# A mixer kernel on one core: the first product of the MLP, for three pairs of token chunks, by seven block products in place of eight

## Chip, cores, metric

The kernel runs on 1 core of one Trainium2 chip. The metric is device time in microseconds (us) of one execution. Before the change the median of 3 runs is 878.2 us (876.82 to 881.63).

## What is computed

Eight sequences of 576 tokens go through windowed attention (8 heads of 64), and the result, 512 wide, through a mixer: a product over the tokens with a ReLU, then an MLP over the channels with a residual. The change is in the MLP, the last three lines.

```python
x = attn_out.transpose(0, 2, 1, 3).reshape(B, S, H * D)   # 8 x 576 x 512
xt = x.transpose(0, 2, 1)
h = np.maximum(xt @ w_tok1, 0.0) @ w_tok2                  # 576 -> 256 -> 576, over tokens
u = x + h.transpose(0, 2, 1)
h2 = np.maximum(u @ w_ch1, 0.0) @ w_ch2                    # 512 -> 1536 -> 512, over channels
return u + h2
```

## The kernel before

**Two stages.** The first stage (to about 283 us) does attention and the token product, writes u to DRAM in 9 chunks of 512 tokens (`u_dram[j]`, 128 partitions x 4 channel tiles x 512 tokens), and converts the weights from float64, in DVE, ACT and POOL work spread over its steps as "jobs". The second stage, from line 539, is the MLP, chunk by chunk (`for j in range(NCHUNK)`, line 585).

**Split numbers.** Every operand of the MLP is held as two float32r tiles, a rounded part `hi` (made by an ACT copy) and the rest `lo` (made by a DVE subtraction, line 94). A product of two such operands is three matmuls: hi by hi, hi by lo, lo by hi.

**A chunk.** The first product, which makes `gp`, goes over 12 tiles `ft` of the 1536 hidden channels. Each is 4 channel tiles x 3 = 12 matmuls of 128x512 into one PSUM bank (line 593). ACT's ReLU takes it out as `ghi` (line 597) and DVE makes `glo` (line 598). The banks come in turn from the tags "s" and "pt", two each, so PE can be four tiles ahead. The second product, `op`, goes over 4 output tiles `ct`, each 12 x 3 = 36 matmuls (line 629), in banks of other tags. DVE adds the residual (line 631) and SP stores the tile (line 632). So a chunk is 144 + 144 matmuls. The last output tile of the last chunk is done in two halves of 256 columns, in two banks (`LAST_PARTS`). The next chunk's u is loaded after tile 3 and split after tile 8 (lines 608 to 611).

**Chunk 0** also holds the rest of the conversion of the second weight matrix: twelve pieces (`late_steps`, line 568, two steps after each tile and seven ahead of each output tile) and three that were kept in DRAM (`load_w2`, `split_w2`). Their DVE work stands in DVE's queue between the `glo` of this chunk.

**Order.** Each engine works its queue in the order in which the program issues it; the schedule is written out by hand. SP issues all DMAs here, in order, and one that waits holds up those behind it.

**Memory.** Pools lie one behind the other, and a pool's tiles follow the order of their first use. A tile that lies where an older tile lay waits for that tile's readers alone (`reuse_waits="tile"`). Pool `pa` (first stage) is followed at the same place by `pb` (MLP).

Of the kernel before, what the change touches and what calls it, by code (L numbers as in the profile page):

```python
# [20 lines left out]
B, H, S, D = 8, 8, 576, 64  # L21
C = H * D
P = 128
# [6 lines left out]
F = 1536  # L30
NCT = C // P
NFT = F // P
NTT = DT // P
TOK = B * S
CHUNK = 512
CW = 384

LAST_PARTS = 2
# [10 lines left out]

NX = 4  # L50
NCHUNK = TOK // CHUNK
NEG = -1.0e9

NEG_PE = -2.0 ** 33
# [20 lines left out]
def mixer_kernel(ctx: ExitStack, tc: tile.TileContext, qh, kh, vh, wt1, wt2, wc1, wc2, out):  # L75
    nc = tc.nc
# [3 lines left out]
    dram = ctx.enter_context(tc.tile_pool(name="dram", bufs=1, space=bass.MemoryType.DRAM))  # L80
    ps = ctx.enter_context(tc.tile_pool(name="ps", bufs=2, space=PSUM))

    ident = const.tile([P, P], F32, name="ident")
    w1hi = const.tile([P, NCT * F], F32R, name="w1hi")
    w1lo = const.tile([P, NCT * F], F32R, name="w1lo")
    w2_dram = dram.tile([P, NFT * C], F32, name="w2_dram")
    u_dram = [dram.tile([P, NCT, CHUNK], F32, name=f"u_dram{j}") for j in range(NCHUNK)]

    def split(eng_hi, eng_lo, hi, lo, src):
        if eng_hi is nc.scalar:  # L90
            nc.scalar.copy(hi, src)  # L91
        else:
            eng_hi.tensor_copy(hi, src)
        eng_lo.tensor_sub(lo, src, hi.bitcast(F32))  # L94

    def load_u(j, pu):
        uf = pu.tile([P, NCT, CHUNK], F32, name=f"uf{j}", tag="uf", bufs=3)
        uhi = pu.tile([P, NCT, CHUNK], F32R, name=f"uhi{j}", tag="uhi", bufs=2)
        ulo = pu.tile([P, NCT, CHUNK], F32R, name=f"ulo{j}", tag="ulo", bufs=2)
# [13 lines left out]
    with ExitStack() as actx:  # L113
# [6 lines left out]
        kbs, loaded, cpool = {}, {}, [pq]  # L120
# [46 lines left out]
        abs_of = {}  # L167

        def job_abs():
            if to_convert:  # L170
                n, raw = to_convert[0]
                m = jobs[n][4]
                abs_of[n] = pb.tile([P, CW], I32, name=f"c{n}", tag="cvc", bufs=2)[:, :m]
                high = raw[:, :m].bitcast(F32).rearrange("p (n t) -> p n t", t=2)[:, :, 1]
                nc.scalar.activation(abs_of[n].bitcast(F32), high, AF.Abs)

# [55 lines left out]
        finished = set()  # L232
# [223 lines left out]
        tok1_plan, n = {}, 0  # L456
        for i in range(TOK1_FROM, NT + 1):
            m = min(n + (1 if i < TOK1_SLOW else 2), i)
            tok1_plan[i] = range(n, m)
            n = m  # L460
        qk(0)
        for i in range(-1, NT + 1):
# [64 lines left out]
            if i == NT - 1:  # L527
# [5 lines left out]
                pu = uctx.enter_context(tc.tile_pool(name="pu", bufs=1, side="right", reuse_waits="tile"))  # L533
                ul = {0: load_u(0, pu)}
# [4 lines left out]
    with ExitStack() as bctx:  # L539
        pb = bctx.enter_context(tc.tile_pool(name="pb", bufs=1, reuse_waits="tile"))  # L540

        w2hi = pb.tile([P, NCT, NFT, P], F32R, name="w2hi")
        w2lo = pb.tile([P, NCT, NFT, P], F32R, name="w2lo")

        w2hf, w2lf = (t.rearrange("p t f c -> p (t f c)") for t in (w2hi, w2lo))
        cpool[0] = pb
        first = [(o, C) for o in range(0, jobs[N_FIRST][3], C)]
        w2_raw = []

        def load_w2():  # L550
            if first:
                o, m = first.pop(0)
                raw = pb.tile([P, C], F32, name=f"raww2_{o}", tag="raww2", bufs=2)
# [31 lines left out]
        for j in range(NCHUNK):  # L585
            uf, uhi, ulo = ul.pop(j)
            g = []
            for ft in range(NFT):
                gp = ps.tile([P, CHUNK], F32, name=f"gp{j}_{ft}", tag=("s", "pt")[ft % 2])
                k = 0  # L590
                for ct in range(NCT):
                    for w, x in ((w1hi, uhi), (w1hi, ulo), (w1lo, uhi)):
                        nc.tensor.matmul(gp, w[:, ct * F + ft * P:ct * F + (ft + 1) * P], x[:, ct], start=(k == 0), stop=(k == 3 * NCT - 1))  # L593
                        k += 1
                ghi = pb.tile([P, CHUNK], F32R, name=f"ghi{j}_{ft}", tag="ghi", bufs=NFT)
                glo = pb.tile([P, CHUNK], F32R, name=f"glo{j}_{ft}", tag="glo", bufs=NFT)
                nc.scalar.activation(ghi, gp, AF.Relu)  # L597
                nc.vector.scalar_tensor_tensor(out=glo, in0=gp, scalar=0.0, in1=ghi.bitcast(F32),  # L598
                                               op0=ALU.max, op1=ALU.subtract)
                g.append((ghi, glo))  # L600
                if j == 0:
                    for _ in range(2):
                        next(late, None)
                    if ft in (1, 2, 7):
                        load_w2()
                    if ft in (6, 8, 10):
                        split_w2()
                if ft == 3 and j + 1 < NCHUNK:
                    ul[j + 1] = load_u(j + 1, pu)
                if ft == 8 and j + 1 < NCHUNK:  # L610
                    split_u(ul[j + 1])
            for ct in range(NCT):
                if j == 0:
                    for _ in range(7):
                        next(late, None)
                    assert all(n in finished for n in range(23 + 4 * ct, 27 + 4 * ct))
                tag, bufs = (("h", 2), ("av", 1), ("h", 2), ("up", 1))[ct]

                n_part = LAST_PARTS if j == NCHUNK - 1 and ct == NCT - 1 else 1
                for part in range(n_part):  # L620
                    cols = slice(part * CHUNK // n_part, (part + 1) * CHUNK // n_part)
                    if part:
                        tag, bufs = ("s", "pt")[part % 2], 2
                    op = ps.tile([P, CHUNK], F32, name=f"op{j}_{ct}_{part}", tag=tag, bufs=bufs)[:, cols]
                    k = 0
                    for ft in range(NFT):
                        ghi, glo = g[ft]
                        for w, x in ((w2hi, ghi), (w2hi, glo), (w2lo, ghi)):
                            nc.tensor.matmul(op, w[:, ct, ft], x[:, cols], start=(k == 0), stop=(k == 3 * NFT - 1))  # L629
                            k += 1  # L630
                    nc.vector.tensor_add(uf[:, ct, cols], op, uf[:, ct, cols])  # L631
                    nc.sync.dma_start(out[j, :, ct, cols], uf[:, ct, cols])


# [36 lines left out]
```

## Time and profile before

| | |
|---|---|
| median of 3 runs | 878.2 us |
| the profiled execution, its own time | 880.53 us |
| its span, first to last instruction | 878.7 us |
| granted TensorE clock, mean | 0.993 |
| DVE busy over the span | 378.3 us (43%) |
| ACT busy over the span | 307.5 us (35%) |
| DMA, mean over the span | 96 GB/s |
| MLP: chunk 0 | 283.4 to 352.6 us |
| MLP: chunks 1 to 8 | 352.6 to 875.3 us |

How to read the rows: a timeline row gives the start, the duration, the engine, the line, the operation and its tiles. A row of groups gives the count, then the busy time and the mean of one in ns. A row of the chain of waits gives the start, the length and the work that the end of the program hung on there. A row of waits gives who waited for whom: total us, times, longest. A row of windows gives the busy time of each engine, then the clock that was granted to PE (PEclk), the DMA engines' busy share and GB/s. Matmuls overlap: PE starts the next one before the last has ended, so their step and not their duration is the price of one.

### The profile page before, as it was taken

The numbers are of one execution on the slowest core, as the hardware profiler recorded it, in microseconds if no ns is written. First come the engines' busy times: TensorE is split into PE (matmuls) and PEld (weight loads), VectorE is DVE, ScalarE is ACT, GpSimd is POOL, SyncE is SP. The second block draws the span as 40 slices with busy tenths as digits, with TensorE's granted clock in tenths as the row PEclk, the third lists the DMA queues.
The fourth block names the chain that finished last, engine by engine and source line by source line (L and its number), as shares of the span: only waits on it lengthen the run. The fifth ranks groups of instructions, "written<-read, shape, count | busy, mean of one in ns | idle before, by whom it ended". The sixth has DMA issues, their size and how long they took to land.

```text
span 878.7 us, 14566 instructions
## 1 busy us (share of the span) xinstructions
PE 850.6 (97%) x6002; PEld 702.6 (80%) x6002; DVE 378.3 (43%) x701; ACT 307.5 (35%) x966; POOL 105.3 (12%) x109
## 2 busy tenths in 40 slices
PE   6889999989989999999999999999999999999998
PEld 4668878868879878888888888888888888888887
DVE  5979878878874795220220220220220220220211
ACT  5778777878875341120120220220220220220200
POOL 3433343433332000000000000000000000000000
PEclk9989999999999999999999999999999999999999
DMA  9566667567535531100100100100100101100001
GB/s 322 195 203 229 200 235 244 183 235 246 182 127 167 182 106 57 60 7 30 60 13 24 60 13 25 60 13 25 60 12 31 54 13 39 46 13 37 0 13 37
DMA packets 39907, 84.69 MB, mean 96 GB/s; under 512 B 5281, under 2 KB 18337, under 8 KB 37921
## 3 DMA queue, kind: packets, MB, share of 16 engines
q1 hardware_dynamic: 37728, 81.93, 27.9%
q10 hardware_dynamic: 2112, 1.84, 0.6%
q8 instruction: 47, 0.77, 0.4%
q14 instruction: 20, 0.16, 0.1%
HBM read 64.09 MB, written 19.66 MB: 95 GB/s over the span
## 4 chain that ended last, share of the span: by engine, by line
PE 83%; DVE 8%; ACT 4%; POOL 2%; issue 2%; DMA 1%; POOLq 0%; SPq 0%; DVEq 0%; ACTq 0%
PE op L629 33%; PE gp L593 30%; PE h L358 5%; PE up L400 4%; PE s L266 4%; PE xp L313 3%; PE up L393 2%; POOL xlo L94 2%; PE pp L301 1%; ACT u L405 1%; DVE r L200 1%; DMA u_dram<-u 1%; DVE c L197 1%; ACT xhi L91 1%; ACT e L294 1%
## 5 line engine op out<-in xcount | busy, mean ns | idle before, releaser
L597 ACT ACTIVATE ghi<-gp 128x512 fp32r<-128x512 f32 x108 | 64.5, 597 | 432.2 <-PE gp L593 431.9
L629 PE MATMUL op<-ghi,w2lo 128*128 128x512 f32 (+1 forms) x444 | 170.9, 385 | 1.9 <-DVE w2lo L94 1.9
L629 PE MATMUL op<-glo,w2hi 128*128 128x512 f32 (+1 forms) x444 | 170.9, 385 | 0.0
L629 PE MATMUL op<-ghi,w2hi 128*128 128x512 f32 (+1 forms) x444 | 170.8, 385 | 0.0
L593 PE MATMUL gp<-ulo,w1hi 128*128 128x512 f32 x432 | 168.1, 389 | 0.0
L593 PE MATMUL gp<-uhi,w1hi 128*128 128x512 f32 x432 | 168.1, 389 | 0.0
L593 PE MATMUL gp<-uhi,w1lo 128*128 128x512 f32 x432 | 168.0, 389 | 0.0
L598 DVE SCALAR_TENSOR_TENSOR glo<-gp,ghi 128x512 fp32r<-128x512 f32 x108 | 74.5, 690 | 187.7 <-ACT ghi L597 187.7
L631 DVE TENSOR_TENSOR uf<-op,uf 128x512 f32<-128x512 f32 (+1 forms) x37 | 25.0, 677 | 243.7 <-PE op L629 243.7
L629 PEld LDWEIGHTS op<-ghi,w2lo 128*128 128x128 f32 x444 | 83.9, 189 | 18.8 <-DVE w2lo L94 2.3
L629 PEld LDWEIGHTS op<-ghi,w2hi 128*128 128x128 f32 x444 | 83.8, 189 | 16.6
L629 PEld LDWEIGHTS op<-glo,w2hi 128*128 128x128 f32 x444 | 83.8, 189 | 16.5
L593 PEld LDWEIGHTS gp<-uhi,w1hi 128*128 128x128 f32 x432 | 81.1, 188 | 16.9
L593 PEld LDWEIGHTS gp<-uhi,w1lo 128*128 128x128 f32 x432 | 81.1, 188 | 16.8
L593 PEld LDWEIGHTS gp<-ulo,w1hi 128*128 128x128 f32 x432 | 81.1, 188 | 16.8
L294 ACT ACTIVATE e<-e,nm 128x128 f32<-128x128 f32 x232 | 90.5, 396 | 8.0 <-DVE nm L286 8.0
L94 POOL TENSOR_TENSOR xlo<-x,xhi 128x512 fp32r<-128x512 f32 x32 | 42.9, 1340 | 66.3 <-ACT xhi L91 66.0
L313 PEld LDWEIGHTS xp<-v,pt 128*64 128x64 f32 x1152 | 37.4, 137 | 16.4 <-ACT pt L303 6.3
L266 PE MATMUL s<-k,q 64*64 64x128 f32 x1152 | 43.7, 287 | 2.4 <-DVE c L197 1.9
L313 PE MATMUL xp<-v,pt 128*64 128x64 f32 x1152 | 43.1, 226 | 2.7 <-ACT pt L303 2.4
L294 ACT ACTIVATION_READ_ACCUMULATOR e<-e,nm 128x1 f32 x232 | 44.8, 193 | 0.0
L303 ACT COPY pt<-pp 128x512 f32<-128x512 f32 x72 | 41.8, 587 | 6.4 <-PE pp L301 6.3
(79 smaller groups left out, 1002.7 us busy)
## 6 DMA issues: line engine op xcount, KB each, us to landing
v<-vh SPq DMA_DIRECT2D x36, 512.0 KB, 3.8
raw<-wc SPq DMA_DIRECT2D x32, 384.0 KB, 4.4
q<-qh SPq DMA_DIRECT2D x36, 256.0 KB, 4.6
k<-kh SPq DMA_DIRECT2D x7, 1280.0 KB, 8.0
out<-uf SPq DMA_DIRECT2D x35, 256.0 KB, 2.3
uf<-u_dram SPq DMA_DIRECT2D x8, 1024.0 KB, 5.6
u_dram<-u SPq DMA_DIRECT2D x7, 512.0 KB, 3.7
k<-kh SPq DMA_DIRECT2D x5, 256.0 KB, 6.2
```

What stands on the lines that cost most here:

```text
L94: eng_lo.tensor_sub(lo, src, hi.bitcast(F32))
L266: nc.tensor.matmul(s[u][half * BLK:(half + 1) * BLK, j], qt[r, j, half], kbs[b][r, j, n * BLK:n * BLK + P], start=not on_pe, stop=True, sk ...
L294: nc.scalar.activation(e[:, h], src[:, h], AF.Exp, bias=nm[:, g:g + 1], scale=by, accum_out=sm[:, g:g + 1])
L303: nc.scalar.copy(pt, pp)
L313: nc.tensor.matmul(xp[half * BLK:(half + 1) * BLK, h], pts[h % 2][:, h // 2, half * BLK:(half + 1) * BLK], vt[:, half, h], start=True, sto ...
L358: nc.tensor.matmul(h_ps[b][tt], w[:, o + tt * P:o + (tt + 1) * P], x, start=first and n == 0, stop=last and n == len(combos) - 1)
L400: nc.tensor.matmul(up[:, :n], hx[:, cs], w[:, tt * S + s0:tt * S + s0 + n], start=False, stop=(k == 6), skip_group_check=True)
L593: nc.tensor.matmul(gp, w[:, ct * F + ft * P:ct * F + (ft + 1) * P], x[:, ct], start=(k == 0), stop=(k == 3 * NCT - 1))
L597: nc.scalar.activation(ghi, gp, AF.Relu)
L598: nc.vector.scalar_tensor_tensor(out=glo, in0=gp, scalar=0.0, in1=ghi.bitcast(F32), op0=ALU.max, op1=ALU.subtract)
L629: nc.tensor.matmul(op, w[:, ct, ft], x[:, cols], start=(k == 0), stop=(k == 3 * NFT - 1))
L631: nc.vector.tensor_add(uf[:, ct, cols], op, uf[:, ct, cols])
```

## The change

Chunks 0, 1 and 2 stay plain; chunks 3 to 8 become three pairs. For a pair, the first product is seen as 2x2 blocks (two halves of the input channels, two halves of the hidden channels, two chunks), and is made from seven block products of sums (Winograd's form of Strassen's) in place of eight. For each pair and each of 6 tiles `f` (`pair_f`) PE does 7 products of 2 x 3 = 6 matmuls into four banks, P, Q, R and S; three of the products add into a bank that DVE or ACT has read in between. The second product is done for two `f` at a time, in eight open banks: 96 matmuls after each two `pair_f`.

The sums of u (`sums`, `sum4`, `prep`) are made on DVE and ACT from raw u tiles, once for each pair, during chunk 2 for the first pair and around the last `pair_f` of a pair for the next. The weights' sums are made once, during chunk 1 (`weight_steps`, two steps after each tile), stored to DRAM (`w1s`), with the three blocks that need no sum, and streamed into three slots that take the place of the first weight matrix in SBUF (`load_w1`, 1.84 MB for each `f` and pair).

Chunks 1 and 2 do the second product in two halves of the hidden channels, with a residual add for each. In the MLP's pool the tiles of the conversion of the second weight matrix move to a pool of their own (`pl`) behind the others. The last output tile is done in two halves of one bank. The first weight matrix is laid out by halves of the hidden channels.

```diff
+N_PLAIN = 3
+NH = NFT // 2
+PRODUCTS = ("m1", "m6", "m7", "m5", "m2", "m4", "m3")
+SLOT, NSLOT = NPROD * 2 * P, 3
...
+    w1s = [dram.tile([P, NH, NPROD, 2, P], F32, name=f"w1s{k}") for k in range(2)]
...
-        cpool[0] = pb
+        gx = (pu.tile([P, 4, CHUNK], F32R, name="ghix", tag="c4", bufs=1),
+              pb.tile([P, 4, CHUNK], F32R, name="glox", tag="c6", bufs=1))
+        gbuf = [(pb.tile([P, CHUNK], F32R, name=f"ghi0_{n}", tag="ghi", bufs=8),
+                 pb.tile([P, CHUNK], F32R, name=f"glo0_{n}", tag="glo", bufs=8)) for n in range(8)]
...
+        pl = tctx.enter_context(tc.tile_pool(name="pl", bufs=1))
+        cpool[0] = pl
...
+        def store_w1(m, k, f0, ct, src):
+            nf = src.shape[1] // P
+            nc.sync.dma_start(w1s[k][:, f0:f0 + nf, PRODUCTS.index(m), ct],
+                              src.bitcast(F32).rearrange("p (f c) -> p f c", c=P))
+
+        def weight_steps():
+            for m, half, ct0 in (("m1", 0, 0), ("m2", 0, 2), ("m4", 1, 2)):
+                for ct in range(2):
+                    for k, w in enumerate((w1hi, w1lo)):
+                        o = (half * NCT + ct0 + ct) * NH * P
+                        store_w1(m, k, 0, ct, w[:, o:o + NH * P])
+            yield
+            nf = CW // P
+            for n in range(2 * NH // nf):
+                ct, f0 = n % 2, n // 2 * nf
...
+                def keep(m, x):
+                    hi, lo = (pw.tile([P, CW], F32R, name=f"w{k}_{m}_{n}", tag=f"w{k}", bufs=4) for k in ("hi", "lo"))
+                    split(nc.scalar, nc.vector, hi, lo, x)
+                    for k, t in enumerate((hi, lo)):
+                        store_w1(m, k, f0, ct, t)
+
+                a = whole("wa", 1, ct)
+                s1 = whole("ws", 1, 2 + ct)
+                yield
+                nc.vector.tensor_add(s1, s1, a)
+                c = whole("wb", 0, ct)
+                keep("m5", s1)
+                yield
+                nc.vector.tensor_sub(a, c, a)
+                nc.vector.tensor_sub(c, s1, c)
+                keep("m7", a)
+                keep("m6", c)
+                yield
+                d = whole("wd", 0, 2 + ct)
+                nc.vector.tensor_sub(d, d, c)
+                keep("m3", d)
+                yield
...
+        def pair_f(q, f):
...
+            if more:
+                sums()
+            for n, m in enumerate(PRODUCTS):
+                b, c = bank[into[m]], comb[q, m]
...
+                        nc.tensor.matmul(b, w[:, at], c[:, h, t], start=(n < 4 and k == 0), stop=(k == 5),
...
+                if m == "m1":
+                    nc.scalar.copy(x1, b)
+                elif m == "m6":
+                    nc.vector.tensor_add(x1, b, x1)
+                elif m == "m7":
+                    nc.vector.tensor_add(x2, b, x1)
+                elif m == "m5":
+                    nc.vector.tensor_add(x3, b, x2)
+                    done(1, f + NH, x3)
+                elif m == "m2":
+                    done(0, f, b)
+                elif m == "m4":
+                    nc.vector.tensor_add(x2, b, x1)
+                    done(0, f + NH, x2)
+                else:
+                    nc.vector.tensor_add(x1, b, x1)
+                    done(1, f, x1)
+                if more:
+                    if m == "m4":
+                        sum4()
+                    prep(q + 1, m, 0)
```

`whole` is one DVE add of 128x384; `split` is one ACT copy and one DVE subtraction; `done` is ACT's ReLU and DVE's `glo`; `more` is true in the last `pair_f` of a pair that another pair follows. `into` puts m1 and m2 into P, m6 into Q, m7 and m4 into R, m5 and m3 into S.

More of the change, by code (lines that the diff above doesn't have):

```diff
@@ L172, in job_abs @@
                 m = jobs[n][4]
-                abs_of[n] = pb.tile([P, CW], I32, name=f"c{n}", tag="cvc", bufs=2)[:, :m]
+                abs_of[n] = cpool[0].tile([P, CW], I32, name=f"c{n}", tag="cvc", bufs=2)[:, :m]
                 high = raw[:, :m].bitcast(F32).rearrange("p (n t) -> p n t", t=2)[:, :, 1]
@@ L552, in load_w2 @@
                 o, m = first.pop(0)
-                raw = pb.tile([P, C], F32, name=f"raww2_{o}", tag="raww2", bufs=2)
+                raw = pl.tile([P, C], F32, name=f"raww2_{o}", tag="raww2", bufs=2)
                 nc.sync.dma_start(raw[:, :m], w2_dram[:, o:o + m])
@@ L583, in mixer_kernel @@
         late = late_steps()
[L585 to L589, printed above, removed]
-                k = 0
-                for ct in range(NCT):
-                    for w, x in ((w1hi, uhi), (w1hi, ulo), (w1lo, uhi)):
-                        nc.tensor.matmul(gp, w[:, ct * F + ft * P:ct * F + (ft + 1) * P], x[:, ct], start=(k == 0), stop=(k == 3 * NCT - 1))
-                        k += 1
[L595 to L632, printed above, removed]
@@ new lines, in w1_at, with relu_split, new_g @@
+        def w1_at(ft, ct):
+            o = (ft // NH * NCT + ct) * NH * P + ft % NH * P
+            return slice(o, o + P)
+        def relu_split(hi, lo, src):
+            nc.scalar.activation(hi, src, AF.Relu)
+            nc.vector.scalar_tensor_tensor(out=lo, in0=src, scalar=0.0, in1=hi.bitcast(F32),
+                                           op0=ALU.max, op1=ALU.subtract)
+        def new_g(name):
+            return tuple(pb.tile([P, CHUNK], F32R, name=f"g{k}{name}", tag=f"g{k}", bufs=8) for k in ("hi", "lo"))
@@ new lines, in gemm1, with gemm2 @@
+        def gemm1(j, ft, u, g):
+            _, uhi, ulo = u
+            gp = ps.tile([P, CHUNK], F32, name=f"gp{j}_{ft}", tag=("s", "pt")[ft % 2])
+            k = 0
+            for ct in range(NCT):
+                for w, x in ((w1hi, uhi), (w1hi, ulo), (w1lo, uhi)):
+                    nc.tensor.matmul(gp, w[:, w1_at(ft, ct)], x[:, ct], start=(k == 0), stop=(k == 3 * NCT - 1))
+                    k += 1
+            relu_split(*g, gp)
+        def gemm2(op, ct, fts, gs, first, last, cols=slice(0, CHUNK)):
+            k = 0
+            for ft, (ghi, glo) in zip(fts, gs):
+                for w, x in ((w2hi, ghi), (w2hi, glo), (w2lo, ghi)):
+                    nc.tensor.matmul(op, w[:, ct, ft], x[:, cols], start=(first and k == 0),
+                                     stop=(last and k == 3 * len(gs) - 1), skip_group_check=not (first and last))
+                    k += 1
@@ new lines, in add_out, with new_op @@
+        def add_out(j, uf, ct, op, final, cols=slice(0, CHUNK)):
+            nc.vector.tensor_add(uf[:, ct, cols], op, uf[:, ct, cols])
+            if final:
+                nc.sync.dma_start(out[j, :, ct, cols], uf[:, ct, cols])
+        OP_TAGS = (("h", 2), ("av", 1), ("h", 2), ("up", 1))
+        def new_op(name, ct):
+            tag, bufs = OP_TAGS[ct]
+            return ps.tile([P, CHUNK], F32, name=f"op{name}_{ct}", tag=tag, bufs=bufs)
+        u = ul.pop(0)
+        for ft in range(NFT):
+            gemm1(0, ft, u, gbuf[ft])
+            for _ in range(2):
+                next(late, None)
+            if ft in (1, 2, 7):
+                load_w2()
+            if ft in (6, 8, 10):
+                split_w2()
+            if ft == 3:
+                ul[1] = load_u(1, pu)
+            if ft == 8:
+                split_u(ul[1])
@@ new lines, in mixer_kernel @@
+        for ct in range(NCT):
+            for _ in range(7):
+                next(late, None)
+            assert all(n in finished for n in range(23 + 4 * ct, 27 + 4 * ct))
+            op = new_op("0", ct)
+            gemm2(op, ct, range(NFT), gbuf, True, True)
+            add_out(0, u[0], ct, op, True)
+        tctx.close()
+        pw = tctx.enter_context(tc.tile_pool(name="pw", bufs=1, reuse_waits="tile"))
+        def store_w1(m, k, f0, ct, src):
+            nf = src.shape[1] // P
+            nc.sync.dma_start(w1s[k][:, f0:f0 + nf, PRODUCTS.index(m), ct],
+                              src.bitcast(F32).rearrange("p (f c) -> p f c", c=P))
@@ new lines, in load_w1, with load_raw @@
+        def load_w1(n):
+            if n < (NCHUNK - N_PLAIN) // 2 * NH:
+                o = n % NSLOT * SLOT
+                for k, w in enumerate((w1hi, w1lo)):
+                    nc.sync.dma_start(w[:, o:o + SLOT].bitcast(F32),
+                                      w1s[k][:, n % NH].rearrange("p m t c -> p (m t c)"))
+        pairs = [(j, j + 1) for j in range(N_PLAIN, NCHUNK, 2)]
+        px = []
+        comb, raws = {}, {}
+        def load_raw(q, t):
+            raws.clear()
+            for name, j, ct in (("r11", 0, t), ("r12", 1, t), ("r22", 1, 2 + t), ("r21", 0, 2 + t)):
+                raws[name] = px[0].tile([P, CHUNK], F32, name=f"{name}_{q}_{t}", tag=name, bufs=1)
+                nc.sync.dma_start(raws[name], u_dram[pairs[q][j]][:, ct])
+            for name in ("t1", "t2"):
+                raws[name] = px[0].tile([P, CHUNK], F32, name=f"{name}_{q}_{t}", tag=name, bufs=1)
@@ new lines, in sums, with sum4, prep @@
+        def sums(t3=True):
+            r = raws
+            nc.vector.tensor_sub(r["t1"], r["r12"], r["r11"])
+            if t3:
+                nc.vector.tensor_sub(r["r12"], r["r22"], r["r12"])
+            nc.vector.tensor_sub(r["t2"], r["r22"], r["t1"])
+        def sum4():
+            nc.vector.tensor_sub(raws["r11"], raws["r21"], raws["t2"])
+        SOURCE = {"m1": "r11", "m6": "t2", "m7": "r12", "m5": "t1", "m2": "r21", "m4": "r11", "m3": "r22"}
+        def prep(q, m, t):
+            if (q, m) not in comb:
+                pool = pb if HOME[m] == "c6" else pu
+                comb[q, m] = pool.tile([P, 2, 2, CHUNK], F32R, name=f"{m}_{q}", tag=HOME[m], bufs=1)
+            c = comb[q, m]
+            split(nc.scalar, nc.vector, c[:, 0, t], c[:, 1, t], raws[SOURCE[m]])
@@ new lines, in mixer_kernel @@
+        steps = weight_steps()
+        for j in range(1, N_PLAIN):
+            u, last = ul.pop(j), j == N_PLAIN - 1
+            if last:
+                tctx.close()
+                px.append(bctx.enter_context(tc.tile_pool(name="px", bufs=1, reuse_waits="tile")))
+                load_raw(0, 0)
+            for half in range(2):
+                g = []
+                for ft in range(half * NH, (half + 1) * NH):
+                    g.append(new_g(f"{j}_{ft}"))
+                    gemm1(j, ft, u, g[-1])
+                    if j == 1:
+                        for _ in range(2):
+                            next(steps, None)
+                    if not last and ft == 3:
+                        ul[j + 1] = load_u(j + 1, pu)
+                    if not last and ft == 8:
+                        split_u(ul[j + 1])
+                    if last:
+                        if ft == 1:
+                            sums()
+                            prep(0, "m1", 0)
+                            prep(0, "m6", 0)
+                        if ft == 2:
+                            prep(0, "m7", 0)
+                            prep(0, "m5", 0)
+                            prep(0, "m2", 0)
+                            load_raw(0, 1)
+                        if ft == 6:
+                            load_w1(0)
+                            sums()
+                        if ft in (7, 8):
+                            for m in (("m1", "m6"), ("m7", "m5", "m2"))[ft - 7]:
+                                prep(0, m, 1)
+                        if ft == 9:
+                            sum4()
+                if last and half == 1:
+                    for m in ("m4", "m3"):
+                        prep(0, m, 1)
+                    load_raw(0, 0)
+                    load_w1(1)
+                    load_w1(2)
+                for ct in range(NCT):
+                    op = new_op(f"{j}_{half}", ct)
+                    gemm2(op, ct, range(half * NH, (half + 1) * NH), g, True, True)
+                    add_out(j, u[0], ct, op, half == 1)
+                    if last and half == 1 and ct == 1:
+                        sums(False)
+                        sum4()
+                        for m in ("m4", "m3"):
+                            prep(0, m, 0)
@@ new lines, in mixer_kernel, with banks, done @@
+        BANKS = ((("s", 2), ("s", 2), ("pt", 2), ("pt", 2)), (("av", 1), ("up", 1), ("h", 2), ("h", 2)))
+        def banks(name, odd):
+            return [ps.tile([P, CHUNK], F32, name=f"{name}_{n}", tag=tag, bufs=bufs)
+                    for n, (tag, bufs) in enumerate(BANKS[odd])]
+        def pair_f(q, f):
+            bank = dict(zip("PQRS", banks(f"gp{q}_{f}", f % 2)))
+            into = {"m1": "P", "m6": "Q", "m7": "R", "m5": "S", "m2": "P", "m4": "R", "m3": "S"}
+            x1, x2, x3 = (px[0].tile([P, CHUNK], F32, name=f"x{n}_{q}_{f}", tag=f"x{n}", bufs=2 if n == 1 else 1)
+                          for n in (1, 2, 3))
+            o = (q * NH + f) % NSLOT * SLOT
+            g = {}
+            def done(c, ft, src):
+                g[c, ft] = new_g(f"{pairs[q][c]}_{ft}")
+                relu_split(*g[c, ft], src)
+            more = f == NH - 1 and q + 1 < len(pairs)
+            if more:
+                sums()
+            for n, m in enumerate(PRODUCTS):
+                b, c = bank[into[m]], comb[q, m]
+                order = (1, 0) if q == 0 and m in ("m4", "m3") else (0, 1)
+                k = 0
+                for t in order:
+                    at = slice(o + (n * 2 + t) * P, o + (n * 2 + t + 1) * P)
+                    for w, h in ((w1hi, 0), (w1hi, 1), (w1lo, 0)):
+                        nc.tensor.matmul(b, w[:, at], c[:, h, t], start=(n < 4 and k == 0), stop=(k == 5),
+                                         skip_group_check=True)
+                        k += 1
+                if m == "m1":
[17 more added lines that the diff above has]
+                    if m == "m4":
+                        sum4()
+                    prep(q + 1, m, 0)
+            return g
@@ new lines, in mixer_kernel @@
+        for q, (ja, jb) in enumerate(pairs):
+            ufs = []
+            final = q == len(pairs) - 1
+            for f0 in range(0, NH, 2):
+                gs = []
+                for f in (f0, f0 + 1):
+                    if f == NH - 2 and not final:
+                        load_raw(q + 1, 0)
+                    gs.append(pair_f(q, f))
+                    load_w1(q * NH + f + NSLOT)
+                    if f == 1:
+                        for j in (ja, jb):
+                            uf = pu.tile([P, NCT, CHUNK], F32, name=f"uf{j}", tag="uf", bufs=2)
+                            nc.sync.dma_start(uf, u_dram[j])
+                            ufs.append(uf)
+                last = f0 == NH - 2
+                if last and not final:
+                    load_raw(q + 1, 1)
+                outs = [(c, ct) for c in range(2) for ct in range(NCT)]
+                ops = banks(f"op{q}_{f0}a", 0) + banks(f"op{q}_{f0}b", 1)
+                for (c, ct), op in zip(outs, ops):
+                    fts = (f0, f0 + NH)
+                    gemm2(op, ct, fts, [gs[0][c, ft] for ft in fts], True, False)
+                if last and not final:
+                    sums()
+                    for m in PRODUCTS:
+                        if m == "m4":
+                            sum4()
+                        prep(q + 1, m, 1)
+                for (c, ct), op in zip(outs, ops):
+                    fts = (f0 + 1, f0 + 1 + NH)
+                    n_part = LAST_PARTS if final and last and (c, ct) == outs[-1] else 1
+                    for part in range(n_part):
+                        cols = slice(part * CHUNK // n_part, (part + 1) * CHUNK // n_part)
+                        gemm2(op[:, cols], ct, fts, [gs[1][c, ft] for ft in fts], False, True, cols)
+                        add_out((ja, jb)[c], ufs[c], ct, op[:, cols], last, cols)
```

17 lines of the change are left out of this document (13 added, 4 removed).

## The prediction

> **What bounds the kernel now.** I read the engines' shares first, then the end of the chain of waits, then the timeline wherever that chain leaves PE.
>
> ```profile
> PE 850.6 (97%) x6002; PEld 702.6 (80%) x6002; DVE 378.3 (43%) x701; ACT 307.5 (35%) x966; POOL 105.3 (12%) x109
> ```
> ```profile
> 323.20 0.69 DVE w2lo L94
> 323.94 28.66 PE op L629 x118
> 352.60 32.64 PE gp L593 x144
> 385.24 32.64 PE op L629 x144
> ...
> 842.20 33.12 PE op L629 x180
> ```
>
> From 323.94 us to the end there is nothing in the chain but PE. A product of 144 matmuls takes 32.64 us, so a matmul costs 32.64/144 = 0.2267 us, in both products alike. Other engines matter only where PE must wait for them. The last row has 108 full matmuls (24.48 us) and 72 of half width in the remaining 8.64 us: 0.12 us each, where half of 0.2267 would be 0.113.
>
> Chunk 0 is the one place where the MLP loses time.
>
> ```profile
> 321.69 0.39 PE L629 MATMUL op<-glo,w2hi 128*128 128x512 f32 x1
> 323.94 0.50 PE L629 MATMUL op<-ghi,w2lo 128*128 128x512 f32 x1 [1.86 <-DVE w2lo L94]
> ```
> ```profile
> 324.00:328.00 4.00, 4.00 (x11) 3.17 (x12) 3.83 (x10) 0.58 (x2) 0.00 (x0) 0.57 0.24 84
> ```
>
> PE sits idle 1.86 us for the last piece of `w2lo`, and then the granted clock is 0.57 for 4 us, in which 11 matmuls run where 17.6 would. Chunk 0's second product starts at 316.0 (chunk start 283.36 + 32.64) and ends at 352.60, 36.6 us against 32.64: 3.9 us lost, 2.0 by the wait and 1.9 by the clock. So a stall of this length costs nearly double here. The Trainium skill ("TensorE: Matmul & The Clock Gate", Part 1) has the clock fall to half after an idle window of about 3.4 us; by that rule alone 1.86 us of idling would cost no clock. The trace differs: it fell after 1.86 us.
>
> **1. Products.** Each pair's first product takes 6 x 7 x 6 = 252 matmuls in place of 288. Three pairs save 108, at 0.2267 us: **-24.5 us**. All lie on the chain. The second product keeps its matmuls.
>
> **2. The seven products' evacuation.** The prices:
>
> ```profile
> L597 ACT ACTIVATE ghi<-gp 128x512 fp32r<-128x512 f32 x108 | 64.5, 597 | 432.2 <-PE gp L593 431.9
> L598 DVE SCALAR_TENSOR_TENSOR glo<-gp,ghi 128x512 fp32r<-128x512 f32 x108 | 74.5, 690 | 187.7 <-ACT ghi L597 187.7
> L631 DVE TENSOR_TENSOR uf<-op,uf 128x512 f32<-128x512 f32 (+1 forms) x37 | 25.0, 677 | 243.7 <-PE op L629 243.7
> ```
> ```profile
> 378.42 2.48 DVE L94 TENSOR_TENSOR ulo<-uf,uhi 128x512 fp32r<-128x512 f32 x4
> ```
>
> One `pair_f` gives PE 42 x 0.2267 = 9.52 us and DVE five adds and four `glo`, 9 x 0.68 = 6.1 us; ACT has five operations of 0.6. DVE, at 64%, does not bound it. The order could: m4 adds into R and must wait for the add that reads m7 from it. m7 ends at 18 x 0.2267 = 4.1 us, its add at about 4.9; m4 starts at 30 x 0.2267 = 6.8. That leaves 1.9 us. m2 and m3 have as much or more. The last `glo` of a `pair_f` ends some 2.8 us into the next one, and that one's m6 add, at 2.9, is in time. The eight banks of the second product are read long before they are needed: the last one, S, is free about 2 us into it and wanted at 42 x 0.2267 = 9.5. I cost the steady state at nothing.
>
> At the two changes of pair, DVE has 11 more operations in the last `pair_f` (three subs first, `sum4`, seven `lo`); four in a row took 2.48 us, so 0.62 each. Its queue is free at 2.8 us, the subs end at 4.7, and then `lo` m1, add m6, `lo` m6, add m7 at 0.65 each end at 7.35: m4 waits 0.55 us. The seven preps after it sit between the two halves of the second product; with the raw u there at about 22 us after the start of that `pair_f` and 11 operations of 0.62, DVE is done with them at 28.8, and the first four banks are free at 31.2, 0.6 us before the next pair needs them at 9.52 + 0.55 + 96 x 0.2267 = 31.8. **+1.1 us** for both, 0 to 6 if the raw u comes later.
>
> **3. Streams in the pairs.** 1.84 MB for each `pair_f`, 3.67 MB in 180 x 0.2267 = 40.8 us: 90 GB/s.
>
> ```profile
> 300.00:310.00 10.00, 10.00 (x46) 8.28 (x45) 9.72 (x22) 5.10 (x11) 0.00 (x0) 1.00 0.77 249
> 15.00:20.00 5.00, 3.96 (x74) 2.93 (x70) 4.34 (x11) 4.18 (x20) 1.80 (x2) 1.00 1.03 414
> ```
>
> At 249 GB/s PE kept its step (46 starts in 10 us), so no cost by sharing memory; at that rate a slot loads in 7.4 us, and the shortest time from a slot's release to its next use is one `pair_f` and one second product, over 30 us. Nothing. If the cover went, a load would cost up to its 7.4 us.
>
> **4. The end.** 12 half-width matmuls in place of 72: 60 x 0.0067 = -0.4 us. But both halves now lie in one bank, so I take it that the second waits for the first one's read.
>
> ```profile
> 875.35 0.42 DVE L631 TENSOR_TENSOR uf<-op,uf 128x256 f32<-128x256 f32 x1 [3.89 <-PE op L629]
> ```
>
> That is 0.42 us and a hop of some 0.2: +0.6. The Trainium skill ("PSUM — Partial Sum Buffer", PSUM bank collisions) wants PE's writes and a read by DVE guarded by bank, not by address; this trace has no two halves in one bank to show it. **+0.2 us** together (-0.4 without the wait).
>
> **5. Chunk 0.** The stall above hangs on DVE's queue, full from 291.82 on; what started it late is
>
> ```profile
> ACT c L175 <- DMA u_dram<-u: 4.3, 1, 4.3
> SPq L217 <- PE up L393: 8.1, 1, 8.1
> ```
> ```profile
> 279.15 1.21 ACTq L420 DMA_DIRECT2D u_dram<-u  x2
> ...
> 282.68 12.35 SPq L217 DMA_DIRECT2D raw<-wc  x4
> ...
> 283.21 0.31 PE L400 MATMUL up<-t2hi,hlo 128*128 128x320 f32 x1
> ...
> 284.02 0.52 ACTq L420 DMA_DIRECT2D u_dram<-u  x1
> ...
> 291.24 0.55 ACT L175 ACTIVATE c<-raw 128x384 f32<-128x384 f32 x1 [4.28 <-DMA u_dram<-u]
> ...
> 291.82 0.36 DVE L187 TENSOR_SCALAR c<-c 128x384 f32<-128x384 f32 x1 [4.13 <-ACT c L175]
> ```
> ```profile
> raw<-wc SPq DMA_DIRECT2D x32, 384.0 KB, 4.4
> ```
>
> Adding up the pools' tiles in order of first use, the first `cvc` tile of pool `pb` lay on the second `ust` buffer, which the last store of u was still reading: that is the wait until 291.24. In the change, pool `pl` starts 88 KB into `pb` (before: the raw tiles at 48 KB). Its `cvc` then lies on the first `ust` buffer, stored some 5 us earlier (279.15 against 284.02), and its raw tiles on the `hhi` and `hlo` tiles that the matmul at 283.21 reads last, 0.8 us later than the raw loads are issued now (282.68, behind the transposes of L393). The raw data should be there at 283.5 + 4.4, about 288, so DVE starts some 3 us earlier. The last `w2lo` (now ended at 323.88, wanted at 321.92) would be 1 us in time. Then the 2.0 us and the 1.9 of the clock both go: **-3.9 us** (0 if I have the layout wrong).
>
> **6. Chunk 1: the weights' sums.** No row of before shows them; I bound them by the nearest.
>
> ```profile
> L202 DVE TENSOR_TENSOR w<-r,c 128x384 f32<-128x384 f32 x12 | 6.7, 557 | 0.4
> L91 ACT CAST w1hi<-w 128x384 fp32r<-128x384 f32 x16 | 8.3, 521 | 0.1
> ```
> ```profile
> 318.95 0.56 DVE L202 TENSOR_TENSOR w<-r,c 128x384 f32<-128x384 f32 x1
> 319.43 0.35 DVE L187 TENSOR_SCALAR c<-c 128x384 f32<-128x384 f32 x1
> ```
>
> Twelve DVE operations of 128x384 for each of four parts, at 0.48 to 0.58 us (the next one starts 0.48 after), and waits for ACT in between: 6.8 us a part. Two steps a tile put about 3.7 us of DVE work per tile, with `glo`, on even tiles and 4.3 on odd, against PE's 2.72. Four banks hide this from the first product, but now the second one starts after six tiles, at 16.3 us, and wants its fifth `glo` at 19.3 and its sixth at 20.0. By the queue these end at 19.4 and 23.2. So 3.2 us, in any case, as the other engines stand.
>
> Then the stores. Twelve at the start hold 4.72 MB in pieces of 512 B, and each part adds 1.57 MB. The sums of the second part overwrite the first part's buffers (`bufs=4`), so ACT and DVE wait there until those have landed, behind all twelve.
>
> ```profile
> 2.00:10.00 8.00, 4.57 (x35) 2.65 (x35) 2.13 (x6) 2.17 (x11) 3.04 (x12) 1.00 0.92 288
> ```
> ```profile
> DMA packets 2508, 2.30 MB, mean 288 GB/s; under 512 B 115, under 2 KB 2020, under 8 KB 2508
> ```
> ```profile
> u_dram<-u ACTq DMA_DIRECT2D x2, 640.0 KB, 5.4
> w_dram<-w SPq DMA_DIRECT2D x4, 192.0 KB, 1.9
> ```
>
> The nearest stretch in size of piece is 2 to 10 us, most of it packets under 2 KB: 288 GB/s, loads though, not stores. The 640 KB stores give the low end, 0.655 MB/5.4 us = 121 GB/s, the 414 above the high one. At 288 the last of the three sums awaited (0.26 MB of output, 4.72 and 1.18 MB) lands at 0.8 (chunk 0's last output add) + 6.16/0.288 + about 1.2 (a 192 KB store's 1.9 less its transfer) = 23.4 us; the fifth `glo` ends at 24.7 and, with the next two steps, the sixth at 28.4. PE waits 24.7 - 19.3 = 5.4, and then 28.4 - 25.4 = 3.0. With 1.9 for the clock, as in chunk 0: **+10 us**. At 414 GB/s the stores are in time and 3.2 + 1.9 = 5 remains; without the clock, 3.2. The Trainium skill ("DMA: Bandwidth & Descriptors", Specifications) has pieces of 512 B run at line rate; if that held against an HBM limit of 358 GB/s it would make this term an estimated 6, inside the range. Load of u for chunk 2 stands behind these stores on SP, with 40 us to spare. In the second half of chunk 1 the 12 operations left over fit under the second product.
>
> Chunk 2's sums are three subs, five or six preps per half and one DMA group, on tiles 1, 2 and 6 to 9; by the same prices they leave the sixth `glo` of either half at about 17.7 us, wanted at 20.0. Nothing.
>
> **The sum.** -24.5 + 1.1 + 0 + 0.2 - 3.9 + 10 = -17.1 us. The profiled execution took 880.53 us (span 878.7); it becomes 863.4. It is 2.3 us above the median of the runs, 878.2; on that scale, in which the forecast stands, 861.1. A difference of less than about 0.5% (4.4 us) can't be told from none.
>
> **The rivals.**
> - *Chunk 1 hardly stalls* (stores at 414 GB/s, no loss of clock): 878.2 - 24.5 + 0.2 - 3.9 + 3.2 + 0.5 = 853.7. For it: the chip moved 414 GB/s at 15 to 20 us. Against: not in pieces that small. 0.17.
> - *Chunk 0 keeps its stall and chunk 1 pays more* (stores at 240 GB/s, a term of 14; changes of pair 2): 869.9. For it: the layout is worked out, not seen. 0.13.
> - *Evacuation binds the pairs.* If each bank's reader came 3 us later than I have it, each of 18 `pair_f` would lose about 1 us: 861.1 + 18 = 879, no change. Against: 1.9 us of slack and DVE at 64%. 0.06.
> - *Slower: the opening stores.* At 121 GB/s the sums land at 53 us, the sixth `glo` comes at 58, and PE waits 38 us: with clock and the other terms 891. It decides from about 160 GB/s down. For it: the 640 KB stores' landing. Against: that landing holds latency and shares its engines. 0.06.
> - *It does not do what it says:* if a load into one slot held up the matmuls that read another (one tile in memory), each of 18 would show its 7 us: about 985. Against it:
>
> ```profile
> 320.69 0.55 DVE L94 TENSOR_TENSOR w2lo<-w,w2hi 128x384 fp32r<-128x384 f32 x1
> ```
>
> This write into `w2lo`, issued ahead of the second product, came after PE had read other parts of the tile (the matmuls up to 321.69): waits go by region. 0.03.
>
> **How the numbers follow.** The likeliest case has 0.55, with its own range 856 to 867 by the rate of the stores. It and the first two rivals make it faster by over 0.5%: 0.85. Evacuation is the same: 0.06. The last two are slower: 0.09. The range takes in the first two rivals and the bounds of parts 2 and 6: 851 to 873, leaving out 0.15 above.
>
> **What would show it.** Right: 42 matmuls in 9.5 us in the pairs with no wait in the chain; in chunk 1 PE waiting for `glo` at the start of the first half's second product, and ACT or DVE waiting for a DMA into `w1s`; no wait for `w2lo` in chunk 0; in the last `pair_f` of a pair a wait of under 1 us for the add into x2. Wrong: DMA waits of PE in the pairs, a clock under 1 there, a wait for `w2lo` as before, or chunk 1 as long as 65.3 us.

## The result and the profile after

The changed kernel takes 866.98 us (median of 4 runs, 866.03 to 869.47) against 879.14 us (median of 4, 876.82 to 881.63): 0.9866 of the time before, 95% interval 0.983 to 0.9901. That is 12.2 us less; the forecast was 17.1 less. The profiled execution took 867.31 us, with a span of 865.5.

The engines' shares, then the end of the chain of waits (three dots stand for rows left out, in the code as well):

```profile
PE 828.6 (96%) x5864; PEld 680.8 (79%) x5864; DVE 527.3 (61%) x939; ACT 336.4 (39%) x1018; POOL 104.8 (12%) x109
```
```profile
323.83 27.07 PE op L628 x118
...
371.46 3.13 DMA w1s<-wlo_m
379.67 15.30 PE op L628 x56
394.97 16.32 PE gp L620 x72
...
427.61 16.32 PE gp L620 x72
...
492.89 19.04 PE gp L839 x84
...
615.92 19.04 PE gp L839 x84
...
738.96 19.04 PE gp L839 x84
```

84 matmuls take 19.04 us, 0.2267 each as before: the products cost what they did, and there are fewer. In chunk 1 the chain leaves PE for a DMA into `w1s`. The stages by their places in the chain:

| stage | before, us | after, us | difference | forecast |
|---|---|---|---|---|
| chunk 0 (from 283.4) | 69.2 | 67.5 | -1.7 | -3.9 |
| chunk 1 | 65.3 | 76.7 | +11.4 | +10 |
| chunk 2 | 65.3 | 65.3 | 0 | 0 |
| chunks 3 to 8, to PE's end | 392.2 | 369.3 | -22.8 | -24.5 + 1.1 + 0.2 |
| sum | | | -13.1 | -17.1 |

The spans differ by 13.2 us. The rows of chunk 1, PE's first:

```profile
375.05 0.79 PE L628 MATMUL op<-ghi,w2hi 128*128 128x512 f32 x1 [5.13 <-ACT ghi L607]
378.04 0.80 PE L628 MATMUL op<-ghi,w2hi 128*128 128x512 f32 x1 [0.92 <-ACT ghi L607]
379.67 0.79 PE L628 MATMUL op<-glo,w2hi 128*128 128x512 f32 x1 [0.84 <-DVE glo L608]
```
```profile
371.25 0.51 ACT L101 CAST whi_m<-ws 128x384 fp32r<-128x384 f32 x1 [6.90 <-DMA w1s<-whi_m]
371.91 0.56 DVE L104 TENSOR_TENSOR wlo_m<-ws,whi_m 128x384 fp32r<-128x384 f32 x1 [5.00 <-DMA w1s<-wlo_m]
374.68 0.56 DVE L104 TENSOR_TENSOR wlo_m<-wb,whi_m 128x384 fp32r<-128x384 f32 x1 [0.56 <-DMA w1s<-wlo_m]
```
```profile
355.59 1.33 SPq L672 DMA_DIRECT2D w1s<-w1hi  x1
356.96 1.34 SPq L672 DMA_DIRECT2D w1s<-w1lo  x1
```

This is the wait that the prediction drew: the second part's sums stand until the first part's stores have landed behind the twelve opening ones (0.393 MB every 1.37 us: 287 GB/s). The third of them was expected 23.4 us into the chunk; it was there 23.8 us after the chain's 350.9. PE then idles 5.13 + 0.92 + 0.84 = 6.9 us.

The row of windows for chunk 1, and one for the ten us in which the granted clock was low:

```profile
350.90:427.60 76.70, 69.77 (x289) 55.97 (x289) 40.04 (x72) 16.53 (x32) 0.00 (x0) 0.93 0.60 171
374.50:384.50 10.00, 7.64 (x15) 4.87 (x16) 8.51 (x16) 3.04 (x7) 0.00 (x0) 0.50 1.02 278
```

Taken in pieces of 0.25 us, the granted clock is 1.00 until 374.25, in the 5.13 us of idling, then 0.50, and 1.00 again from 384.75: half speed for 10.2 us. Of the 11.4 us lost, the 4.5 that are not idle time are nearly all slow steps in that stretch: PE is busy in 7.64 of the 10 us shown, at half its rate.

In chunk 0 the wait for `w2lo` is still there:

```profile
284.03 3.50 DMA u_dram<-u
```
```profile
287.68 7.21 SPq L227 DMA_DIRECT2D raw<-wc  x4
...
291.10 0.55 ACT L185 ACTIVATE c<-raw 128x384 f32<-128x384 f32 x1 [4.12 <-DMA raw<-wc]
...
323.83 0.50 PE L628 MATMUL op<-ghix,w2lo 128*128 128x512 f32 x1 [1.74 <-DVE w2lo L104]
```

The first row is from the chain: the last store of u lands at 287.53. The raw loads go out at 287.68, five us later than before. But this time the clock did not fall after the wait (1.00 from 324.3 to 328.3, where it was 0.57 before), and 118 matmuls took 27.07 us where they took 28.66.

In the pairs, the only waits of PE over 0.3 us are one in the last `pair_f` of each of the first two pairs, and one between the two halves of the last output tile:

```profile
591.15 0.73 PE L839 MATMUL gp<-m,w1hi 128*128 128x512 f32 x2 [0.34 <-DVE x L847]
...
861.22 0.39 PE L628 MATMUL op_4b<-ghi,w2hi 128*128 128x256 f32 x1 [0.52 <-DVE uf L633]
```

A pair takes 615.92 - 492.89 = 123.03 us, of which 540 x 0.2267 = 122.4 are matmuls.

### The profile page after: what moved, and what is told of

It reads as the page before. It is cut to its first block, busy times and chain, and to the rows that moved or that the text cites. A ratio compares the mean times of both kernels' runs of the same rounds, so it can differ in the third digit from the quotient of the medians.

```text
span 865.5 us, 14815 instructions
## 1 busy us (share of the span) xinstructions
PE 828.6 (96%) x5864; PEld 680.8 (79%) x5864; DVE 527.3 (61%) x939; ACT 336.4 (39%) x1018; POOL 104.8 (12%) x109
## 3 DMA queue, kind: packets, MB, share of 16 engines
q10 hardware_dynamic: 2112, 1.84, 0.6%
## 4 chain that ended last, share of the span: by engine, by line
PE 77%; DVE 10%; ACT 4%; SPq 2%; issue 2%; POOL 2%; DMA 2%; POOLq 0%; DVEq 0%; ACTq 0%
PE gp L839 18%; PE op L628 11%; PE gp L620 6%; PE h L368 5%; PE up L410 4%; PE s L276 4%; PE op_4a L628 4%; PE op_2b L628 4%; PE op_2a L628 4%; PE op_0b L628 4%; PE op_0a L628 4%; PE op_4b L628 4%; PE xp L323 3%; PE up L403 2%; SPq L672 2%
## 5 line engine op out<-in xcount | busy, mean ns | idle before, releaser
L839 PE MATMUL gp<-m,w1hi 128*128 128x512 f32 x504 | 155.4, 389 | 0.7 <-DVE x L847 0.7
L839 PEld LDWEIGHTS gp<-m,w1hi 128*128 128x128 f32 x504 | 94.5, 188 | 20.9 <-DVE x L847 1.5
L839 PE MATMUL gp<-m,w1lo 128*128 128x512 f32 x252 | 98.0, 389 | 0.0
L843 ACT COPY x<-gp 128x512 f32<-128x512 f32 x18 | 10.4, 578 | 143.8 <-PE gp L839 143.8
L628 PE MATMUL op<-ghi,w2hi 128*128 128x512 f32 x128 | 51.4, 401 | 6.0 <-ACT ghi L607 6.0
L620 PE MATMUL gp<-ulo,w1hi 128*128 128x512 f32 x144 | 56.0, 389 | 0.0
L620 PE MATMUL gp<-uhi,w1hi 128*128 128x512 f32 x144 | 56.0, 389 | 0.0
L620 PE MATMUL gp<-uhi,w1lo 128*128 128x512 f32 x144 | 56.0, 389 | 0.0
L839 PEld LDWEIGHTS gp<-m,w1lo 128*128 128x128 f32 x252 | 47.3, 188 | 9.9
L628 PE MATMUL op<-glo,w2hi 128*128 128x512 f32 x128 | 51.3, 401 | 0.9 <-DVE glo L608 0.8
L628 PE MATMUL op<-ghi,w2lo 128*128 128x512 f32 x128 | 51.0, 398 | 0.0
```

The source lines that it names most:

```text
L620: nc.tensor.matmul(gp, w[:, w1_at(ft, ct)], x[:, ct], start=(k == 0), stop=(k == 3 * NCT - 1))
L628: nc.tensor.matmul(op, w[:, ct, ft], x[:, cols], start=(first and k == 0), stop=(last and k == 3 * len(gs) - 1), skip_group_check=not (fir ...
L839: nc.tensor.matmul(b, w[:, at], c[:, h, t], start=(n < 4 and k == 0), stop=(k == 5), skip_group_check=True)
```

## The experiments

The theory was: fewer matmuls on a PE that bounds the MLP (-24.5), with two separate stalls around it, one in chunk 0 by a wait of the conversion pool, one in chunk 1 by the weights' sums, and there two causes, the stores' backlog and DVE's own work. The rivals: one cause for chunk 1 alone; the pairs bound by the readers of the banks.

**An eighth product.** Each `pair_f` makes m1 twice, the second time over the first.

```diff
-                k = 0
-                for t in order:
+                for _ in range(2 if m == "m1" else 1):
+                  k = 0
+                  for t in order:
```

> Each pair_f makes its first product m1 twice, the second time over the first, so PE has 8 x 6 = 48 matmuls again in place of 42; nothing else is changed. Theory (PE bounds the pairs): 18 x 6 x 0.2267 = 24.5 us more, all in the pairs, 131.2 us for a pair in place of 123.0. Rival (the banks' readers on ACT and DVE bound the pairs, or the stream of weights): less than half of that, the added matmuls run where PE waited.

890.06 us (one run). In the chain:

```profile
492.40 21.76 PE gp L840 x96
...
622.96 21.76 PE gp L840 x96
```

96 matmuls in 21.76 us, and 622.96 - 492.40 = 130.56 us for a pair, which is 576 x 0.2267 with nothing left over. The span is 22.8 us longer than the changed kernel's: 24.5, less the 0.6 us waits at the two changes of pair, which went, less 1 us that chunk 1 happened to lose less, and 0.6 us by which the MLP began later. (The half clock of chunk 1 began 2.7 us ahead of the first product after the wait, in the changed kernel 0.7 us: 2 us more of it fell into idling.) So the products' term is PE's step and their count. With eight products in place, the rest of the change costs 11.6 us: 890.06 against 878.43 for the kernel before, measured beside it.

**The conversion pool's waits.**

```diff
-        pl = tctx.enter_context(tc.tile_pool(name="pl", bufs=1))
+        pl = tctx.enter_context(tc.tile_pool(name="pl", bufs=1, reuse_waits="tile"))
```

> The pool of the second weight matrix's conversion tiles waits tile by tile for the first stage, in place of for all of it. My theory of chunk 0's stall (the raw loads wait for the last store of u, which their tiles do not touch): the raw loads are issued at about 284 us in place of 287.7, DVE's queue starts some 2 to 3 us earlier, PE's wait for w2lo at 322 us (2.1 us with its gap) goes, and chunk 0's second product starts and ends 2 us earlier; the run takes about 2 us less. Rival: the raw loads and the last store of u share the DMA engines, so the raw data comes no earlier, and the wait stays at 1.7 us.

865.4 us (one run). SP's row and PE's:

```profile
283.59 9.19 SPq L227 DMA_DIRECT2D raw<-wc  x4
```
```profile
322.38 0.50 PE L628 MATMUL op<-ghix,w2lo 128*128 128x512 f32 x1
```

The raw loads now wait for PE's `up` (line 410), the product whose last matmul stood at 283.21 in the kernel before, as the layout says. DVE starts at 287.79 in place of 291.69, and the wait falls from a gap of 2.12 us to 0.50 (0.2267 of it is the step). Chunk 0 is 1.6 us shorter. So the pool's wait was the cause; `pl` was opened without waits by tile and stood until the last store of u had landed. In the total, 1.6 us is less than the changed kernel's own runs differ by (866.03 to 869.47); the experiment with both edits, below, shows it clear of that.

**The opening stores last.** The loop over m1, m2 and m4 in `weight_steps` goes behind the sums, with its `yield`, so the sums also begin one step earlier.

```diff
-            for m, half, ct0 in (("m1", 0, 0), ("m2", 0, 2), ("m4", 1, 2)):
...
-            yield
             nf = CW // P
...
                 keep("m3", d)
                 yield
+            for m, half, ct0 in (("m1", 0, 0), ("m2", 0, 2), ("m4", 1, 2)):
...
+            yield
```

> The twelve opening stores are issued after the sums of chunk 1, not ahead of them. Theory (two causes, DMA backlog ahead of the sums' stores and DVE's own work): the waits of ACT and DVE for w1s (6.9 and 5.0 us at the second part) go, DVE's work alone keeps the sixth glo late by about 3 us, so chunk 1 takes 65.3 + 3.2 to 5.5 = 68.5 to 71 us in place of 76.7, and the run 6 to 8 us less. Rival 1, all of it is the backlog: chunk 1 takes 65 to 66 us, 11 less. Rival 2, the sums' own stores are too slow by themselves: chunk 1 stays over 74.

862.06 us (ratio to before 0.9815, interval 0.98 to 0.9831), 4.9 less than the change, where 6 to 8 was expected. Chunk 1 takes 71.6 us (first product's start to the next chunk's), 5.1 less, just over the 68.5 to 71 expected. ACT and DVE no longer wait for `w1s`. PE still waits, for the fifth and the sixth tile:

```profile
370.81 0.50 PE L628 MATMUL op<-ghi,w2hi 128*128 128x512 f32 x1 [1.26 <-ACT ghi L607]
371.53 0.50 PE L628 MATMUL op<-glo,w2hi 128*128 128x512 f32 x1 [0.23 <-DVE glo L608]
374.14 0.49 PE L628 MATMUL op<-ghi,w2hi 128*128 128x512 f32 x1 [1.88 <-ACT ghi L607]
374.87 0.50 PE L628 MATMUL op<-glo,w2hi 128*128 128x512 f32 x1 [0.23 <-DVE glo L608]
```

Both rivals fall: neither is the backlog all of it, nor are the sums' own stores too slow. What is left are 3.6 us of idle (3.2 forecast) that DVE's own work makes; chunk 1 loses 6.3 us, the rest mostly by slow steps, in a stretch of 3.4 us at half the clock that holds this row:

```profile
375.50:378.50 3.00, 3.00 (x8) 2.31 (x7) 2.51 (x5) 1.19 (x3) 0.00 (x0) 0.50 1.05 324
```

**One step at a time.**

```diff
                     if j == 1:
-                        for _ in range(2):
-                            next(steps, None)
+                        next(steps, None)
...
                     add_out(j, u[0], ct, op, half == 1)
+                    if j == 1:
+                        next(steps, None)
```

> One step of the weights' sums after each of the twelve tiles and one after each of the eight output tiles of chunk 1, in place of two after each tile; the stores stay first. Theory: DVE has some 2.4 us of work for each 2.72 us tile, and the second part's sums come after the opening stores have landed (about 18 us into the chunk), so both waits go: chunk 1 takes 65.3 to 66 us, 10.5 to 11.4 less, and the run about 856. Rival: the DMA backlog alone is the cause and still reaches the first half's second product: chunk 1 keeps 4 us or more of its wait.

855.66 us (0.9739, interval 0.9723 to 0.9754), 11.3 less than the change. Chunk 1 in the chain has no wait:

```profile
350.95 16.32 PE gp L620 x72
367.27 16.32 PE op L628 x72
383.59 16.32 PE gp L620 x72
399.91 16.32 PE op L628 x72
```

65.28 us, as in the kernel before. The same sums and the same stores, in the same order, cost nothing once DVE's work per tile is under PE's 2.72 us (some 2.4 by the estimate above) and the buffers are asked for when the opening stores have all but landed: DVE waits 0.60 us there at 373.61, PE not at all.

**Both.** `one_step` and `pl_tile` together.

> One step of the weights' sums per tile and per output tile, and the conversion pool's waits tile by tile, together. Theory (the two stalls are independent): one_step's 855.7 us less the 1.7 us that pl_tile took off, 854; no wait of PE for w2lo, ghi or glo over 0.5 us is left before the first pair. Rival: chunk 1's DVE queue takes the gain of chunk 0 back, 855.7 as without.

853.91 us (0.9713, interval 0.9693 to 0.9733). Chunks 0 and 1:

```profile
283.20:348.90 65.70, 65.57 (x290) 53.95 (x289) 50.27 (x106) 22.63 (x44) 0.00 (x0) 1.00 0.38 122
348.90:414.20 65.30, 65.30 (x290) 54.07 (x289) 40.37 (x72) 16.88 (x32) 0.00 (x0) 1.00 0.69 201
```

Chunk 1 is at its 288 x 0.2267 = 65.3 us. Chunk 0 takes 65.9, from its first product at 283.17 to chunk 1's at 349.06, so 0.6 us is left there. The runs of this kernel (853.57 to 854.38) lie wholly below those of `one_step` (855.1 to 855.92), so the pool's 1.7 us is real. The total is 24.9 us under the kernel before, measured beside it (878.81), and 13 under the change.

**Longer pieces in the stores.** The layout of `w1s` puts one product's six tiles side by side; the slices of the stores and the loads follow it.

```diff
-    w1s = [dram.tile([P, NH, NPROD, 2, P], F32, name=f"w1s{k}") for k in range(2)]
+    w1s = [dram.tile([P, NPROD * 2, NH, P], F32, name=f"w1s{k}") for k in range(2)]
```

> The changed kernel with another layout of the weights' sums in DRAM: the stores of chunk 1 go in pieces of 3072 and 1536 B, the loads in the pairs in pieces of 512 B. Theory (the backlog of the twelve opening stores is set by the size of the pieces): the stores take 1.0 to 1.1 us each in place of 1.34, the twelve end 3 to 4 us earlier, and chunk 1 takes 73 to 74 us in place of 76.7; the pairs, which have over 30 us for a load, stay at 123.0 us. Rival (any store of this size goes at some 300 GB/s): no change in chunk 1.

861.35 us (0.9804, interval 0.9778 to 0.983). The opening stores:

```profile
355.41 0.95 SPq L672 DMA_DIRECT2D w1s<-w1lo  x1
356.40 0.95 SPq L672 DMA_DIRECT2D w1s<-w1hi  x1
```

One every 0.99 us, 397 GB/s against 287. Chunk 1 takes 70.6 us, 6.1 less, where 73 to 74 us was expected: ACT and DVE no longer wait for `w1s`, PE idles 2.8 us in chunk 1, no more than DVE's own work left in `stores_last`, and the clock is at half for 3.4 us in place of 10.2. So in these stores the longer piece gave the higher rate. The pairs take 123.08 us with their loads in pieces of 512 B: the two loads of a slot land after 5.8 and 8.4 us in place of 4.8 and 6.6, and that costs nothing.

**More work for DVE in the pairs.** Four or eight more adds in each `pair_f`.

```diff
                     nc.vector.tensor_add(x1, b, x1)
+                    for _ in range(4):
+                        nc.vector.tensor_add(x3, x1, x1)
                 elif m == "m7":
```

> Four more DVE adds of 128x512 in each pair_f, into a tile that is written over later, between the adds that read m6 and m7. Theory (PE bounds, with 1.8 us between the end of m7's add and the start of m4): 4 x 0.6 = 2.4 us, of which 0.6 fall into time in which DVE was idle, so the 16 ordinary pair_f lose 0 to 0.2 us each and the two last ones of a pair, whose DVE queue is full, up to 2.4 each: 2 to 8 us more than the changed kernel's 867. Rival (the readers bound the pairs): 18 x 2.4 = 43 us more.

> Eight more such adds. Theory: m7's add ends 4.8 - 0.6 = 4.2 us later, 2.4 us after m4 could start, so each of 18 pair_f is 2.4 us longer: 43 us more than the changed kernel (35 to 55). If the slack is larger than I count, under 25.

892.8 us and 964.95 us (one run each): 26 and 98 more than the changed kernel, where 2 to 8 and 43 were expected. Both expectations fell, and so did the rival's 43 for the first. With four, PE's rows in the first two `pair_f` and in the last one of the first pair, and DVE's:

```profile
499.62 0.73 PE L839 MATMUL gp<-m,w1hi 128*128 128x512 f32 x2 [0.28 <-DVE x L849]
...
510.68 0.73 PE L839 MATMUL gp<-m,w1hi 128*128 128x512 f32 x2 [1.24 <-DVE x L849]
...
599.28 1.22 PE L839 MATMUL gp<-m,w1hi 128*128 128x512 f32 x2 [4.19 <-DVE x L849]
```
```profile
496.10 2.87 DVE L847 TENSOR_TENSOR x<-x 128x512 f32<-128x512 f32 x4
498.88 0.68 DVE L849 TENSOR_TENSOR x<-gp,x 128x512 f32<-128x512 f32 x1
...
505.82 0.69 DVE L608 SCALAR_TENSOR_TENSOR glo<-x,ghi 128x512 fp32r<-128x512 f32 x1 [0.76 <-ACT ghi L607]
506.43 0.68 DVE L845 TENSOR_TENSOR x<-gp,x 128x512 f32<-128x512 f32 x1
507.15 2.87 DVE L847 TENSOR_TENSOR x<-x 128x512 f32<-128x512 f32 x4
```

Four adds into the same tile hold the next operation back by 2.78 us (496.10 to 498.88), 0.70 each and not 0.6. And the delay is handed on: the second `pair_f` of each two begins its m6 add only after the first one's last `glo`, and so PE waits 1.24 us there and 0.28 in the first. At each change of pair it waits 4.19 us, and the clock is at half for 3.4 us after it. In all PE idles 18.5 us for that add; the rest is the clock and the slower start after each wait. With eight, PE's idle for that add is 63.5 us in all and the mean clock over the run 0.956, so part of the 98 us is clock. The slack of 1.9 us that the prediction worked out is right for one `pair_f` (in the changed kernel m7's add ends at 507.22, m4 is due at 509.05), but a delay uses it up in the second of two. This is also a test of the prediction's third rival, readers some 3 us late: it priced that at 1 us for each `pair_f`, and 2.78 us late cost 25.5/18 = 1.4. PE bounds the pairs, by less than it looks with DVE busy 64.6 of 123 us there.

## Why the prediction was right, and where it was off

The time lies near the top of the likeliest case's 856 to 867. The kernel that came is a mixture, though: chunk 0 keeps its wait, as in the second rival, and the prediction's own sign of being wrong, a wait for `w2lo` as before, appeared.

- **The mechanism and the products** held: 108 matmuls at 0.2267 us, shown by the chain and by the added eighth product.
- **The pairs' evacuation, streams and changes of pair**: nothing, nothing and 1.1 forecast; 0, 0 and 1.3 measured, in the last `pair_f` and on the add that was named. The end of the kernel, +0.2 forecast, cost 0.4: PE does wait for the read of the first half's bank, and the wait cost some 0.8 us with the slower start after it, where 0.6 was forecast. The hop of 0.2 us in that forecast had no row behind it.
- **Chunk 1** was forecast at +10 with its two causes and cost 11.4. The idle time was less than forecast (6.9 against 8.4) and the clock more (4.5 against 1.9): I took one fall of the clock as in chunk 0, where it lasted 3.4 us, and here it lasted 10.2, through two more waits. The two misses cancel in part, so that 11.4 comes as near to 10 as it does is partly luck. In the other four runs that have these waits chunk 1 lost 10.4 to 11.3 us. That both causes are real is shown by `stores_last`, which takes the backlog away alone (5.1 us less, 3.6 of idle left), and `one_step`, which takes both (11.4 less).
- **Chunk 0** is the step that failed: -3.9 forecast, -1.7 measured, and even that is luck: the wait stayed, at 1.74 us, and only the clock did not fall this time. The layout was read rightly, but I took it that the new pool waits tile by tile as its neighbours do. The diff has it without `reuse_waits`; so the raw loads stood for the last store of u, to 287.68. With waits by tile they went out at 283.59, and 1.6 us came back. The condition was in the diff line, and I did not price it.
- The remaining gap between -13.1 in the profiles and -12.2 in the medians is within what runs of one kernel differ by.

What makes the clock fall after a wait is not settled. In chunk 0 it fell in the kernel before, after 1.86 us of idle; in seven later runs, after 1.52 to 1.74 us at the same place, it did not. In chunk 1 it fell in every run in which PE waited there: after two waits close together (1.26 and 1.88 us, or 1.41 and 1.13), or inside the idle of 5.13 us itself, ahead of the two waits that follow. The Trainium skill ("TensorE: Matmul & The Clock Gate", Part 1) has an idle window of about 3.4 us that runs freely; the 5.13 us case agrees, the cases of under 3.4 us do not, and no run here was made to tell why. How long it stays low is plainer: in pieces of 0.25 us, each of these stretches was 3.4 us at half the clock after the waits of under 2 us, and 10.2 us, three times as long, after the idle of 5.1.

## What to carry to other kernels

Work that is added beside a bound engine must be priced twice: by its sum, and by the place where the bound engine first asks for something that stands behind it in a queue. Here the same sums and stores cost 11.4 us at two steps a tile and nothing at one. And when an edit opens a new pool of buffers, read what it waits for, as for any new instruction.

## What the runs showed of the hardware that I had not expected

Stores to DRAM of 0.393 MB went at 287 GB/s in pieces of 512 B and at 397 GB/s in pieces of 3072 B. The Trainium skill ("DMA: Bandwidth & Descriptors", Specifications) gives 512 B as enough for line rate; for these stores it was not. The prediction's 288, from loads, was right for the shorter pieces, and the 358 that it set as a limit in one estimate was passed by the longer ones.

Four DVE adds of 128x512 that write the same tile held the next operation back by 2.78 us, 0.70 each; where the next operation writes another tile it started after 0.61 (the `glo` at 505.82, the add at 506.43). That the common tile is the reason was not tested.
